# Opening of a fused attention, dense and expert kernel: y held in PSUM between quarters, a new order of single steps, and three element-wise steps moved to GpSimd

## The chip, the cores and the metric

The kernel runs on one core of a Trainium2 chip. The metric is the device time of one execution in microseconds. The engines are TensorE (PE, matrix products; PEld is its weight load), VectorE (DVE), ScalarE (ACT), GpSimd (POOL) and SyncE (SP, whose queue issues most transfers). Each engine works through its own queue in order; a wait at the head of a queue holds everything behind it on that engine.

## The reference

Three stages follow one another on 4608 tokens (8 batches of 576, 512 columns each). All inputs are fp32 except the dense weights, which arrive with eight bytes each and are read as pairs of 32-bit words.

```
kv  = einsum('bhsd,bhse->bhde', k, v)              # attention without softmax, 8 heads of 64
out = einsum('bhsd,bhde->bhse', q, kv)
x   = out / sqrt(mean(out*out) + 1e-6) * g_norm    # 4608 x 512
h   = x @ w_in                                     # 512 -> 2048
g   = max(h, 0) + alpha * min(h, 0)
y   = g @ w_out                                    # 2048 -> 512
e   = argmax(y @ w_gate);  gate = softmax(...)[e];  eom = sigmoid(y @ w_output_gate)
out = gate * eom[e] * (max(y @ w1[e], 0) @ w2[e])  # 8 experts, one for each token
```

## The kernel before

The tokens are cut into 12 blocks of 384, each of three tiles of 128 tokens. A value that feeds a product is held as two fp16 parts (a high part, and the rest as a low part), and each product is a sum of three fp16 products of parts.

The **opening** handles blocks 0 and 1 together, because the dense weights are not yet in SBUF. The weights come in 16 pieces of w_in and 16 of w_out (512 KB each), and are worked up in four **quarters** of four pieces. Each piece takes: a magnitude on ACT (`magnitude`, L493), a row maximum on DVE (`maximum`, L500, tile acc), three bit steps on DVE that build an fp32 value out of the two words (`bits`, L508, L510, L512), and, when the scale of the quarter is known, a high part on ACT (L533) and a low part on DVE (L535). The scale takes a reduction on DVE (tile amx), a transpose on PE (L152, tile allmax), a reduction on DVE (tile amrow), a product with ones on PE (L159), and a run of tiny steps on DVE (`pow2`, tiles pw_e, sig). Of a quarter's h, each of eight pieces (four for each block) takes twelve products on PE (L663), a scaled copy out of PSUM on ACT (L666, tile m), the bent line on DVE (L672, tile r), a high part on ACT (L674, tile g) and a low part on GpSimd (L675). Six **y units** follow (L686: twelve products into one PSUM bank, one for each block and tile), and ACT copies each sum out of PSUM (L716). From the second quarter on, a y unit begins with an fp32 product of the sum so far with a scaled identity, `keep` (L711), which brings the sum back into PSUM with the factor that fits the quarter's scale.

The order of the opening is written out by hand, the same on every engine: code calls the steps one after another, in larger groups (a piece's maximum and bits in one call, a whole scale in two). Behind it, the fourth quarter's y units, the routing of blocks 0 and 1 and the attention of block 2 are interleaved by the framework's scheduler.

For **later blocks** (3 to 11) attention takes, for each tile, a scaling of q by powers of two on DVE (L321, tile qs), its high part on ACT and its low part on DVE (L325), a transposing transfer (tile qT), products on PE (L347), a square on ACT, a row sum on DVE, a power -1/2 on GpSimd (L369, tile rs), a scaling on DVE (L394), and the high part (ACT, L401) and low part (DVE, L406) of x, and a transposing transfer. The k-v product of each batch is scaled in the same way (L291, tile kvsc). GpSimd also scatters the finished rows of y (L813, ytab). After block 11 the expert stage runs on tiles of tokens sorted by expert (L1140, L1162).

Of the kernel before, what the change touches and what calls it, by code (L numbers as in the profile page):

```python
# [66 lines left out]
def body(ctx: ExitStack, tc, q, k, v, g_norm, w_in, w_out, alpha, w_gate, w_og, w1, w2, out):  # L67
# [79 lines left out]
    def all_max(am, nm):  # L147
        return max_rows(max_turn(am, nm, ps_l, "l"), am.shape[1], nm)

    def max_turn(am, nm, pool_, tag):  # L150
        ps = pool_.tile([P, P + E], F32, tag=tag, name="allmax" + nm)
        pe.transpose(ps[:am.shape[1], 0:P], am, ident)  # L152
        return ps

    def max_rows(ps, n, nm):
# [18 lines left out]
    keep = const.tile([P, P], F32, name="keep")  # L174
# [42 lines left out]
    late = []  # L217

    def load_kv(n, now=False):
        if not now and late is not None:  # L220
            late.append(lambda: load_kv(n, True))
        elif n < len(kv_order):
# [11 lines left out]
    def load_q(n, now=False):  # L234
        if not now and late is not None:
            late.append(lambda: load_q(n, True))
        elif n < len(q_order):
# [24 lines left out]
    def kv_step(n, pool_=None, tag="a"):  # L262
# [4 lines left out]
        if hp % 2 == 0:  # L267
            kv_ps[b] = (pool_ or ps_a).tile([P, 2, D], F32, tag=tag, name=f"kvps_{b}_{hp}")
        ps = kv_ps[b]
# [4 lines left out]
        if hp % 2 == 1:  # L274
            for i in range(2):
                sl = slice(64 * i, 64 * i + 64)
                (act.copy if b < 2 else dve.tensor_copy)(out=kvbd[b % 2][sl, hp - 1:hp + 1, sl], in_=ps[sl])
        load_kv(n + 2 if n >= NPAIR else len(kv_order))
# [3 lines left out]
    def kv_halves(b):  # L282
# [8 lines left out]
        dve.tensor_tensor(out=t, in0=src, in1=s_.unsqueeze(2).to_broadcast([P, H, D]), op=ALU.mult)  # L291
# [5 lines left out]
    def att_parts(i):  # L297
# [6 lines left out]
        def tr(t, pool_=None, tag="a"):  # L304
# [3 lines left out]
            if split_q:  # L308
# [12 lines left out]
                dve.tensor_tensor(out=qs, in0=qv, in1=s_.unsqueeze(2).to_broadcast([P, H, D]), op=ALU.mult)  # L321
# [6 lines left out]
            else:  # L328
                qps = (pool_ or ps_a).tile([P, NPAIR, P], F32, tag=tag, name="qps" + nm)
                for hp in range(NPAIR):  # L330
                    for e in range(2):
                        pe.matmul(qps[64 * e:64 * e + 64, hp, :], qv[:, 2 * hp + e, :], ident, start=True, stop=True)
                qT[t] = at.tile([P, NPAIR, P], F32, tag="qT", name="qT" + nm)
                act.copy(out=qT[t], in_=qps)
# [3 lines left out]
        def products(t):  # L338
# [12 lines left out]
            xs = at.tile([P, DM], F32, tag="xs", name="xs" + nm, bufs=3)  # L351
# [34 lines left out]
        def scaled(t):  # L386
            nm = f"_{G}_{t}"
# [4 lines left out]
            else:  # L392
# [3 lines left out]
                              in1=rs.unsqueeze(2).to_broadcast([P, H, D]), op=ALU.mult)  # L396
            if i < 2 and t == ts[-1]:
# [6 lines left out]
        def low(t):  # L404
            xs, x16 = tiles.pop(t)
            dve.tensor_tensor(out=x16[:, 1, :], in0=xs, in1=x16[:, 0, :], op=ALU.subtract)  # L406
# [5 lines left out]
        return ts, tr, products, sums, exponents, scaled, low  # L412

    def att_steps(i):
        G = i // 3
        split_q = i >= SPLIT_Q
        ts, tr, products, sums, exponents, scaled, low = att_parts(i)

        def om(t):
            products(t)  # L420
            sums(t)
            exponents(t, t)
            scaled(t)
            low(t)
# [126 lines left out]
    def scale_out(j, am=None):  # L551
# [8 lines left out]
        else:  # L560
# [7 lines left out]
            exp_to(d[:, 1:2], d[:, 1:2], 127 << 23)  # L568
            act.activation(out=keep, in_=ident, func=AF.Copy, scale=d[:, 1:2])
        if j == NG - 1:  # L570
            d = small.tile([P, NG], F32, tag="egf", name="egf", bufs=1)
# [630 lines left out]
    with tc.manual_schedule(engines={ET.PE, ET.DVE, ET.Activation, ET.SP}):  # L1202
# [23 lines left out]
        for n in range(2):  # L1226
            kv_step(n)
# [266 lines left out]
```

## Time and profile before

| | us |
|---|---|
| median of three runs | 1390.82 (1384.95 to 1391.77) |
| the profiled execution, its own time | 1392.61 |
| its span in the trace | 1390.6 |
| PE, DVE, ACT, POOL busy in it | 1287.6, 821.6, 556.9, 251.1 |
| mean granted TensorE clock | 0.975 of 2.4 GHz |

The span is the time from the first to the last instruction; the execution's own time is 2.0 us longer. Busy shares are means over stages with different limits, so the stages are read one by one below.

### The profile page before, as it was taken

The numbers are of one execution on the slowest core, as the hardware profiler recorded it, in microseconds if no ns is written. First come the engines' busy times: TensorE is split into PE (matmuls) and PEld (weight loads), VectorE is DVE, ScalarE is ACT, GpSimd is POOL, SyncE is SP. The second block draws the span as 40 slices with busy tenths as digits, with TensorE's granted clock in tenths as the row PEclk, the third lists the DMA queues.
The fourth block names the chain that finished last, engine by engine and source line by source line (L and its number), as shares of the span: only waits on it lengthen the run. The fifth ranks groups of instructions, "written<-read, shape, count | busy, mean of one in ns | idle before, by whom it ended". The sixth has DMA issues, their size and how long they took to land. (4 is left out here: it accounts for less than half of the span.)

```text
span 1390.6 us, 21985 instructions
## 1 busy us (share of the span) xinstructions
PE 1287.6 (93%) x7717; PEld 666.1 (48%) x7717; DVE 821.6 (59%) x2386; ACT 556.9 (40%) x931; POOL 251.1 (18%) x342
## 2 busy tenths in 40 slices
PE   5688879999999999999999999999979999999995
PEld 4443435555555454545555555554434444444442
DVE  6786877867878687869697878462521221212210
ACT  3443535435556474646564656351111111111110
POOL 3212203111120102110111111101322222222110
PEclk9799999999999999999999999999989999999998
DMA  9562215646896775677846665316999799799631
GB/s 255 148 174 91 70 52 150 146 83 191 202 240 174 218 183 148 198 199 160 237 117 177 174 174 146 99 32 179 246 329 192 164 281 281 144 253 234 130 84 38
DMA packets 323297, 236.22 MB, mean 170 GB/s; under 512 B 246236, under 2 KB 279020, under 8 KB 318704
## 3 DMA queue, kind: packets, MB, share of 16 engines
q1 hardware_dynamic: 303760, 189.05, 55.3%
q0 software_dynamic: 8960, 28.91, 6.5%
q10 hardware_dynamic: 10464, 16.82, 3.8%
q8 instruction: 62, 1.02, 0.3%
q14 instruction: 51, 0.42, 0.1%
HBM read 248.34 MB, written 53.25 MB: 217 GB/s over the span
## 5 line engine op out<-in xcount | busy, mean ns | idle before, releaser
L663 PE MATMUL h<-x,wi 128*128 128x384 f16 x2304 | 406.6, 328 | 12.0 <-ACT m L666 10.1
L686 PE MATMUL y<-wo,g 128*128 128x512 f16 x1728 | 404.0, 382 | 13.6 <-ACT wo L533 5.3
L663 PEld LDWEIGHTS <-wi 128*128 128x128 f16 x2304 | 221.2, 98 | 163.9 <-issue 17.5
L686 PEld LDWEIGHTS <-g 128*128 128x128 f16 x1728 | 165.8, 98 | 210.4 <-issue 25.3
L1146 DVE CAST h_d<-br_d 128x512 f16<-128x512 f32 x62 | 27.1, 438 | 267.9 <-ACT br_d L1144 160.1
L1162 PE MATMUL bo_d<-lane,hT_d 128*128 128x512 f16 x744 | 169.4, 385 | 10.4 <-DMA hT_d<-h_d 10.4
L1140 PE MATMUL bh_d<-lane,byT_d 128*128 128x512 f16 x744 | 165.3, 379 | 0.0
L672 DVE SCALAR_TENSOR_TENSOR r<-m,alphat 128x384 f32<-128x384 f32 x192 | 119.6, 625 | 30.1 <-ACT m L666 28.9
L369 POOL TENSOR_TENSOR rs<-ms,mhalf 128x8 f32<-128x8 f32 x36 | 65.9, 1833 | 358.7 <-DVE qm L375 330.1
L674 ACT CAST g<-r 128x384 f16<-128x384 f32 x192 | 97.1, 508 | 83.9 <-DVE r L672 80.6
L1162 PEld LDWEIGHTS <-hT_d 128*128 128x128 f16 x744 | 73.4, 99 | 102.1 <-DMA hT_d<-h_d 11.4
L1140 PEld LDWEIGHTS <-byT_d 128*128 128x128 f16 x744 | 72.7, 98 | 88.1 <-issue 0.8
L666 ACT ACTIVATE m<-h,scal 128x384 f32<-128x384 f32 x160 | 91.6, 575 | 44.6 <-PE h L663 43.5
L675 DVE TENSOR_TENSOR g<-r,g 128x384 f16<-128x384 f32 x160 | 88.1, 551 | 15.3 <-ACT g L674 14.8
L454 ACT ACTIVATE whi_w<-rawe,es_w 128x1024 f16<-128x1024 f32 x64 | 71.2, 1143 | 56.0 <-DVE es_w L144 40.5
L455 DVE SCALAR_TENSOR_TENSOR wlo_w<-rawe,es_w,whi_w 128x1024 f16<-128x1024 f32 x64 | 81.0, 1278 | 20.8 <-DMA ws<-wlo_w 17.8
L1144 ACT ACTIVATE br_d<-bh_d 128x512 f32<-128x512 f32 x62 | 37.0, 597 | 131.2 <-PE bh_d L1140 109.9
L813 POOL DMA_INDIRECT ytab<-row,pos x36 | 38.8, 1077 | 277.8 <-DVE pos L794 65.9
L602 ACT ACTIVATE eab_w<-rawe 128x1024 bf16<-128x1024 f32 x64 | 67.5, 1057 | 40.6 <-DMA rawe<-in_moe_w_dram 36.9
L1165 ACT ACTIVATE ob_d<-bo_d,msc_d 128x512 f32<-128x512 f32 x31 | 21.3, 687 | 143.2 <-PE bo_d L1162 143.2
L1166 POOL DMA_INDIRECT out_dram<-ob_d,oidx_d x31 | 32.5, 1050 | 215.8 <-ACT ob_d L1165 208.9
L675 POOL TENSOR_TENSOR g<-r,g 128x384 f16<-128x384 f32 x32 | 32.9, 1032 | 146.0 <-ACT g L674 146.0
(350 smaller groups left out, 1284.9 us busy)
## 6 DMA issues: line engine op xcount, KB each, us to landing
lane<-ws SPq DMA_DIRECT2D x150, 1024.0 KB
rawe<-in_moe_w_dram SPq DMA_DIRECT2D x64, 512.0 KB
ws<-whi_w ACTq DMA_DIRECT2D x64, 256.0 KB
ws<-wlo_w SPq DMA_DIRECT2D x64, 256.0 KB
rawwi<-in_moe_w_in_dram SPq DMA_DIRECT2D x16, 512.0 KB
q<-in_q_dram SPq DMA_DIRECT2D x16, 512.0 KB
rawwo<-in_moe_w_out_dram SPq DMA_DIRECT2D x16, 512.0 KB
k<-in_k_dram SPq DMA_DIRECT2D x28, 256.0 KB
```

The source lines that it names most:

```text
L369: pool.tensor_tensor(out=rs, in0=ms, in1=mhalf, op=ALU.pow)
L454: act.activation(out=dst_h, in_=src, func=AF.Copy, scale=s)
L455: dve.scalar_tensor_tensor(out=dst_l, in0=src, scalar=s, in1=dst_h, op0=ALU.mult, op1=ALU.subtract)
L602: act.activation(out=ab.rearrange("p a b -> p (a b)"), in_=raws[4 * m + i], func=AF.Abs)
L663: pe.matmul(ps, wi[:, f // 4 * NC + c, w, fs], xt[i][:, xc, :], start=(n == 0), stop=(n == 3 * NC - 1))
L666: act.activation(out=r0, in_=ps, func=AF.Copy, scale=(scst if start else scal)[:, f:f + 1])
L672: dve.scalar_tensor_tensor(out=r, in0=r0, scalar=alphat[:, f:f + 1], in1=r0, op0=ALU.mult, op1=ALU.max)
L674: act.copy(out=hi, in_=r)
L675: (pool if start else dve).tensor_tensor(out=lo, in0=r, in1=hi, op=ALU.subtract)
L686: pe.matmul(ps, g[:, t, f % GF, us], wo[:, f, w, :], start=(start and m == 0), stop=(stop and m == 2))
L1140: pe.matmul(hp[ts], j["yT"][:, x, ts], w1_[:, w, c, hs], start=(m == 0), stop=(m == 3 * NC - 1))
L1162: pe.matmul(po[ts], hT[:, g, ts], w2_[:, w, f, :], start=(m == 0), stop=(m == 3 * NFE - 1))
```

## The change

Four things change.

- **y in PSUM.** The six y sums of blocks 0 and 1 get a PSUM bank each from the first quarter on (three of the pool of attention, two of the pool of y, one of the small pool). The products of the next quarter add to what stands there. Between quarters ACT scales a bank in place (`y_scaled`, F). The products with `keep` and the copies between quarters are gone; one copy (L1376 of the changed kernel) remains after the fourth quarter. h takes turns in two fixed banks.
- **Order.** The opening is a list of some 470 words, each a single step, issued in the order of the list. Quarters use g tiles 2, 3 and 0, 1 in turn. Attention of both blocks 0 and 1 stands ahead of the first h products.
- **Loads.** All of k, v and q of the first tiles stand ahead of the first weight in SP's queue.
- **GpSimd.** For every block from 3 on, the scaling of q, the low part of x, and for every batch from 2 on the scaling of the k-v product, go from DVE to GpSimd.

```
-        ps = ps_y.tile([P, DM], F32, tag="y", name=f"y_{i}_{j}_{u}")
-        if j:
-            pe.matmul(ps, keep, acc[:, u, :], start=True, stop=False)
+        if j == 0:
+            pool_, tag = ((ps_a, "a"), (ps_y, "y") if u < 2 else (ps_l, "l"))[i]
+            ybank[i, u] = pool_.tile([P, DM], F32, tag=tag, name=f"y_{i}_{u}")
         for f in range(j * GF, (j + 1) * GF):
-            y_products(ps, g, f, u, j == 0 and f == 0, f == (j + 1) * GF - 1)
+            y_products(ybank[i, u], gs2[j, i], f, u, f == 0, f % GF == GF - 1,
+                       skip_group_check=True)
             if j == NG - 1:
                 tick()
-        act.copy(out=acc[:, u, :], in_=ps)
+
+    def y_scaled(i, j, u):
+        act.activation(out=ybank[i, u], in_=ybank[i, u], func=AF.Copy, scale=kfac[:, j:j + 1])
...
-            act.activation(out=keep, in_=ident, func=AF.Copy, scale=d[:, 1:2])
+            exp_to(kfac[:, js], d[:, 1:2], 127 << 23)
...
-                dve.tensor_tensor(out=qs, in0=qv, in1=s_.unsqueeze(2).to_broadcast([P, H, D]), op=ALU.mult)
+                pool.tensor_tensor(out=qs, in0=qv, in1=s_.unsqueeze(2).to_broadcast([P, H, D]), op=ALU.mult)
...
-            dve.tensor_tensor(out=x16[:, 1, :], in0=xs, in1=x16[:, 0, :], op=ALU.subtract)
+            (dve if i < SPLIT_Q else pool).tensor_tensor(out=x16[:, 1, :], in0=xs, in1=x16[:, 0, :], op=ALU.subtract)
...
-        dve.tensor_tensor(out=t, in0=src, in1=s_.unsqueeze(2).to_broadcast([P, H, D]), op=ALU.mult)
+        pool.tensor_tensor(out=t, in0=src, in1=s_.unsqueeze(2).to_broadcast([P, H, D]), op=ALU.mult)
...
+    plan = """
+    f0 f1 N0 Li0 Li1 Li2 N1 Li3 Lo0 n4 n5 k0 k1 k2 K1 Ai0 q0 Mi0 Bi0 Ai1 q1 Q0 k3 Q1 N2 Mi1 Lo1 Ai2 Bi1 q2 K3
...
+    G132 R031 Y122 G031 Y121
+    """
...
+        for word in plan.split():
+            emit(word)
...
+            y_scaled(i, NG - 1, u)
+            y_unit(i, NG - 1, u)
+            act.copy(out=accs[i][:, u, :], in_=ybank[i, u])
```

In the list, L, A, M, B, S and T are load, magnitude, maximum, bits, high and low part of a weight piece (i for w_in, o for w_out); U, u, V, v, W are the five steps of a scale; H, C, R, G are products, copy, bend and split of an h piece (block, quarter, number); Y and F are a y unit and its scaling (block, quarter, tile).

**SP, the start of the program.** These rows are SP's first loads before the change (wi stands in for k and v at this time, rawwi is a weight piece, q_0 the first q):

```order
L255 DMA wi<-in_k_dram 64x8x64
L258 DMA wi<-in_k_dram 128x4x256
L255 DMA wi<-in_v_dram 64x8x64
L258 DMA wi<-in_v_dram 128x4x256
L478 DMA rawwi_238<-in_moe_w_in_dram 128x1024
L258 DMA wi<-in_k_dram 128x4x256
L258 DMA wi<-in_v_dram 128x4x256
L478 DMA rawwi_242<-in_moe_w_in_dram 128x1024
L242 DMA q_0_244<-in_q_dram 128x8x128
L478 DMA rawwi_246<-in_moe_w_in_dram 128x1024
```

And these are the first of the changed program:

```order
L244 DMA wi<-in_k_dram 64x8x64
L247 DMA wi<-in_k_dram 128x4x256
L244 DMA wi<-in_v_dram 64x8x64
L247 DMA wi<-in_v_dram 128x4x256
L247 DMA wi<-in_k_dram 128x4x256
L247 DMA wi<-in_v_dram 128x4x256
L231 DMA q_0_264<-in_q_dram 128x8x128
L492 DMA rawwi_266<-in_moe_w_in_dram 128x1024
L492 DMA rawwi_268<-in_moe_w_in_dram 128x1024
L492 DMA rawwi_270<-in_moe_w_in_dram 128x1024
```

The first weight piece moves from fifth to eighth place, behind the second half of k and v and the first q, and three weight pieces now follow each other.

**DVE, the scale of w_in's second quarter.** Before the change, the row reduction (amrowwi) is followed at once by the first step that needs PE's product with ones (pw_ewi):

```order
L1221 TENSOR_REDUCE amxwi_1287<-accwi_1224 128x1
L508 TENSOR_SCALAR cwi_1306<-uwi_1284 128x512
L510 SCALAR_TENSOR_TENSOR cwi_1306<-rawwi_1100,cwi_1306 128x512
L512 SCALAR_TENSOR_TENSOR wo<-rawwi_1100,cwi_1306 128x512
L157 TENSOR_REDUCE amrowwi_1327<-allmaxwi_1289 1x1
L132 TENSOR_SCALAR pw_ewi_1330<-allmaxwi_1289 128x1
L135 TENSOR_SCALAR pw_ewi_1330<-pw_ewi_1330 128x1
```

In the changed program the same two steps (amrowi, and pw_ewi from an h bank) stand eight rows apart:

```order
L1261 TENSOR_REDUCE amrowi_887<-hbank_671 1x1
L696 SCALAR_TENSOR_TENSOR r_3_889<-m_3_839,alphat 128x384
L549 SCALAR_TENSOR_TENSOR wo<-wi,sogs,wo 128x512
L514 TENSOR_SCALAR uwo_891,accwo_880<-uwo_891 128x512
L696 SCALAR_TENSOR_TENSOR r_0_915<-m_0_897,alphat 128x384
L522 TENSOR_SCALAR cwo_917<-uwo_891 128x512
L524 SCALAR_TENSOR_TENSOR cwo_917<-rawwo_831,cwo_917 128x512
L526 SCALAR_TENSOR_TENSOR wi<-rawwo_831,cwo_917 128x512
L132 TENSOR_SCALAR pw_ewi_936<-hbank_671 128x1
L135 TENSOR_SCALAR pw_ewi_936<-pw_ewi_936 128x1
```

Two bends of h and the bits of a w_out piece now stand between the reduction and the step that waits for PE.

**POOL, the first later block.** Before the change GpSimd has only the powers (rs) and the scatter of y's rows (ytab, row) around block 3:

```order
L369 TENSOR_TENSOR rs_8_2120<-ms_8_2118,mhalf 128x8
L369 TENSOR_TENSOR rs_0_2670<-ms_0_2668,mhalf 128x8
L813 DMA ytab<-row_193,pos_2362 36864x528
L813 DMA ytab<-row_194,pos_2362 36864x528
L810 COPY row_193<-ids 128x1
L813 DMA ytab<-row_195,pos_2362 36864x528
L810 COPY row_194<-ids 128x1
```

In the changed program the scalings (kvsc, qs) and the low part of x (x_1_0) stand among them:

```order
L375 TENSOR_TENSOR rs_8_2043<-ms_8_2041,mhalf 128x8
L285 TENSOR_TENSOR kvsc_2170<-kvbd_205,kvs_2157 128x512
L327 TENSOR_TENSOR qs_0_2365<-q_0_1970,qsc_0_2358 128x512
L327 TENSOR_TENSOR qs_1_2458<-q_0_1970,qsc_1_2451 128x512
L327 TENSOR_TENSOR qs_2_2645<-q_2_2023,qsc_2_2638 128x512
L843 DMA ytab<-row_193,pos_2282 36864x528
L375 TENSOR_TENSOR rs_0_2589<-ms_0_2587,mhalf 128x8
L843 DMA ytab<-row_194,pos_2282 36864x528
L840 COPY row_193<-ids 128x1
L415 TENSOR_TENSOR x_1_0_2599<-xs_0_2580,x_1_0_2599 128x512
```

The scatter of block 0's rows now stands behind four element-wise steps, and the low part of x stands behind a wait for a scattered row.

## Rows read from the trace of the kernel before

**Rows 1.** Windows, four stages: length, then each engine's busy us (instructions), clock, DMA, GB/s

```profile
0.00:213.70 213.70, 161.52 (x956) 91.02 (x957) 157.62 (x377) 95.06 (x174) 45.64 (x86) 0.91 0.46 130
213.70:247.40 33.70, 31.68 (x258) 17.88 (x257) 24.80 (x75) 16.04 (x28) 8.09 (x6) 1.00 0.58 157
247.40:960.00 712.60, 690.19 (x4490) 374.24 (x4491) 537.53 (x1666) 373.29 (x612) 104.93 (x108) 1.00 0.64 168
960.00:1390.60 430.60, 404.22 (x2018) 182.93 (x2015) 101.69 (x271) 72.51 (x117) 92.42 (x143) 0.97 0.81 193
```

**Rows 2.** Windows within the opening; columns PE, PEld, DVE, ACT, POOL as above

```profile
0.00:11.20 11.20, 3.02 (x29) 2.28 (x30) 4.10 (x26) 1.93 (x2) 5.90 (x50) 1.00 0.78 221
...
116.20:164.40 48.20, 39.63 (x187) 19.51 (x187) 35.61 (x77) 21.38 (x40) 8.24 (x8) 0.96 0.27 88
164.40:213.70 49.30, 41.32 (x198) 20.61 (x198) 39.05 (x89) 22.97 (x42) 9.76 (x10) 0.97 0.15 49
```

**Rows 3.** Waits in the opening, 0 to 213.7: total us, times, longest

```profile
DVE r L672 <- ACT m L666: 15.1, 9, 5.6
DVE pw_ewi L132 <- PE allmaxwi L159: 14.4, 2, 7.3
...
PE allmaxwi L152 <- DVE amxwi L1221: 12.4, 4, 5.3
...
DVE uwi L500 <- ACT uwi L493: 5.5, 3, 3.4
...
DVE uwo L500 <- ACT uwo L493: 4.6, 2, 2.5
```

**Rows 4.** Timeline of DVE, second quarter of w_in: start, us, [idle before, releaser]

```profile
132.17 0.27 DVE L157 TENSOR_REDUCE amrowwi<-allmaxwi 1x1 f32<-1x128 f32 x1
139.71 0.16 DVE L132 TENSOR_SCALAR pw_ewi<-allmaxwi 128x1 int32<-128x1 int32 x1 [7.27 <-PE allmaxwi L159]
```

**Rows 5.** Timeline of PE at the same place

```profile
136.61 2.75 PE L686 MATMUL y<-wo,g 128*128 128x512 f16 x12
139.29 0.38 PE L159 MATMUL allmaxwi<-amrowwi,ones 1*128 1x1 f32 x2
```

**Rows 6.** Groups by line: PE in the opening, ACT in the last stage (PSUM source)

```profile
L711 PE MATMUL y<-g,keep 128*128 128x512 f32 x24 | 14.2, 679 | 0.0
...
L1165 ACT ACTIVATE ob_d<-bo_d,msc_d 128x512 f32<-128x512 f32 x31 | 21.3, 687 | 143.2 <-PE bo_d L1162 143.2
```

**Rows 7.** DMA rate in 40 slices of 0 to 215; DVE's first weight step

```profile
GB/s 129 303 352 297 273 222 173 288 231 231 9 2 99 222 236 383 86 3 105 188 98 3 0 129 208 53 0 111 181 102 0 0 156 212 24 3 0 0 0 142
...
11.26 0.69 DVE L500 TENSOR_SCALAR_CACHE_REDUCE uwi<-uwi 128x512 f32<-128x512 f32 x1 [0.27 <-ACT uwi L493]
```

**Rows 8.** GpSimd's 384-column low part; a DVE step beside it, and alone

```profile
L675 POOL TENSOR_TENSOR g<-r,g 128x384 f16<-128x384 f32 x30 | 30.9, 1032 | 142.4 <-ACT g L674 142.4
...
120.70 0.92 POOL L675 TENSOR_TENSOR g<-r,g 128x384 f16<-128x384 f32 x1 [1.70 <-ACT g L674]
...
120.72 1.18 DVE L508 TENSOR_SCALAR cwi<-uwi 128x512 int32<-128x512 int32 x1
...
127.79 0.43 DVE L508 TENSOR_SCALAR cwi<-uwi 128x512 int32<-128x512 int32 x1
```

**Rows 9.** The middle, 247.4 to 960: DVE groups that move, POOL's waits, PE's waits

```profile
L406 DVE TENSOR_TENSOR x<-xs,x 128x512 f16<-128x512 f32 x27 | 18.5, 686 | 4.0 <-ACT x L401 3.9
L321 DVE TENSOR_TENSOR qs<-q,qsc 128x512 f32<-128x512 f32 x27 | 18.4, 683 | 0.0
...
POOL ytab L813 <- DMA ytab<-row,pos: 35.4, 13, 4.2
...
PE h L663 <- ACT m L666: 7.6, 8, 2.1
PE ops L347 <- DMA qT<-q: 5.2, 4, 1.9
PE y L686 <- ACT g L674: 4.6, 3, 3.9
```

**Rows 10.** Timeline of PE around the start of block 2

```profile
215.30 1.09 PE L332 MATMUL qps<-ident,q 128*64 128x128 f32 x16
...
236.92 1.09 PE L350 MATMUL ops<-kvbd,qT 128*64 128x128 f32 x16
...
247.38 0.82 PE L663 MATMUL h<-x,wi 128*128 128x384 f16 x4 [1.91 <-DMA x<-x]
```

More of the change, by code (lines that the diff above doesn't have):

```diff
@@ L173, in body @@
         "sig", "isig", "sog", "isog", "scol", "crow"))
[L174 removed]
+    kfac = const.tile([P, NG], F32, name="kfac")
     eg = const.tile([P, NG], F32, name="eg")
@@ L215, in body, with load_kv @@
     q_order = [(G, t) for G in range(B // 2) for t in (0, 2, 4, 6, 8)]
[L217 to L222, printed above, removed]
+    def load_kv(n):
+        if n < len(kv_order):
             b, hp = kv_order[n]
@@ L232, in load_kv, with load_q @@
                 kv_in[nm, n] = t
[L234 to L237, printed above, removed]
+    def load_q(n):
+        if n < len(q_order):
             G, t = q_order[n]
@@ L328, in tr @@
             else:
[L329 to L334, printed above, removed]
+                turned(t)
+                turned_copy(t)
             if t % 2 == 1 or t == 8:
@@ L410, in low @@
                                    in_=x16.rearrange("p a b -> p (a b)"))
-        return ts, tr, products, sums, exponents, scaled, low
+        return ts, dict(q=turned, Q=turned_copy, t=tr, p=products, P=squares, s=sums, e=exponents, x=scaled, X=high, z=low,
+                        Z=x_turned)
     def att_steps(i):
@@ L416, in att_steps @@
         split_q = i >= SPLIT_Q
-        ts, tr, products, sums, exponents, scaled, low = att_parts(i)
+        ts, do = att_parts(i)
+        tr = do["t"]
         def om(t):
[L420 to L424, printed above, removed]
+            for what in "pPs":
+                do[what](t)
+            do["e"](t, t)
+            for what in "xXzZ":
+                do[what](t)
         nxt = {0: 2 * G + 1, 1: None, 2: 2 * G + 2}[i % 3]
@@ L669, in h_unit, with h_bend @@
     def h_unit(f, g, start, part):
+        h_split(f, g, start, h_bend(f, part))
+    def h_bend(f, part):
         i, r0 = part
@@ new lines, in body, with weights, scales @@
+    ybank, hbank, held = {}, [], {}
+    dense = dict(i=din, o=dout)
+    parts = {}
+    for i in range(2):
+        ts, do = att_parts(i)
+        for t in ts:
+            parts[t] = do
+    def weights(what, d, n):
+        if what == "L":
+            d.load(n)
+        elif what == "A":
+            d.magnitude(n)
+        elif what == "M":
+            d.maximum(n)
+        elif what == "B":
+            d.bits(n)
+        else:
+            d.split(n, "ST".index(what))
+    def scales(what, w, j):
+        d, nm = dense[w], f"{w}{j}"
+        if what == "U":
+            held[nm] = small.tile([P, 1], F32, tag="amx", name="amx" + nm)
+            dve.tensor_reduce(out=held[nm], in_=d.acc, axis=AX.X, op=ALU.max)
+        elif what == "u":
+            if j:
+                ps = hbank["io".index(w)][:, BLK:BLK + P]
+            else:
+                ps = ps_l.tile([P, P], F32, tag="l", name="allmax" + nm)
+            pe.transpose(ps[:1, :], held[nm], ident)
+            held[nm] = ps
+        elif what == "V":
+            m = small.tile([E, 1], F32, tag="amrow", name="amrow" + nm)
+            dve.tensor_reduce(out=m[:1], in_=held[nm][:1, :], axis=AX.X, op=ALU.max)
+            held[nm] = held[nm], m
+        elif what == "v":
+            ps, m = held[nm]
+            held[nm] = ps[:, 0:1]
+            pe.matmul(held[nm], ones32[:1, :], m[:1], start=True, stop=True)
+        else:
+            (scale_in, scale_out)["io".index(w)](j, held.pop(nm))
@@ L1217, in body @@
         dve.tensor_tensor(out=sgp, in0=gp, in1=sal, op=ALU.mult)
-        def top(d, nm):
-            m = small.tile([P, 1], F32, tag="amx", name="amx" + nm)
-            dve.tensor_reduce(out=m, in_=d.acc, axis=AX.X, op=ALU.max)
-            return max_turn(m, nm, ps_l, "l")
-        (t0, t1, t2), tr, products, sums, exponents, scaled, low = att_parts(0)
-        din.magnitude(0)
-        for n in range(2):
-            kv_step(n)
-        din.build(0)
-        din.magnitude(1)
-        for n in range(2, NPAIR):
-            kv_step(n)
```

325 lines of the change are left out of this document (123 added, 202 removed).

## The prediction

> **What bounds the kernel now.** I read the windows by stage first. From 247 us to 960 us PE is busy 690.2 of 712.6 us, and in the last stage 404.2 of 430.6 us; there PE is the bound, and little is left to win [rows 1]. In the opening (0 to 213.7 us, the last h product) no engine is the bound: PE is busy 161.5, DVE 157.6 and ACT 95.1 of 213.7 us [rows 1]. Quarters of it look alike: 48 to 49 us long with 40 to 41 us of PE and 36 to 39 us of DVE [rows 2]. So PE and DVE, both in order, wait for each other in turn, and the list of waits says where. DVE waits 15.1 us in sum for ACT's copies of h, 14.4 us for PE's product with ones, 5.5 and 4.6 us for magnitudes; PE waits 12.4 us for the reductions of w_in's scales [rows 3]. One place shows the mechanism. DVE finishes the row reduction at 132.4 us and stands still for 7.27 us until PE's product with ones [rows 4]; that product takes 0.38 us, but stands behind y units in PE's queue and starts at 139.29 us [rows 5]. Before that PE had itself waited for DVE. It is an order of steps that costs here, more than the work.
>
> **The new order.** I build the new end of the opening from DVE, the engine whose work hardly changes. All its steps of the opening stay in it, so 157.6 us of busy time remain [rows 1]. To it come:
>
> - *The start.* DVE now has 4.1 us of work before its first weight step at 11.26 us [rows 2, 7]. In the new order of loads the first weight has 2.9 MB before it in SP's queue (k and v of batch 0 with 2.36 MB, q with 0.52 MB) instead of 1.3 MB, so that it ends at 3.4 MB. The rate row gives 0.7 MB in the first 5.4 us, 2.3 MB after 10.8 us, and then 352 GB/s [rows 7], so 3.4 MB are there at 13.9 us; with about 1 us of landing and 0.7 us of magnitude DVE starts at about 15.6 us. Idle before: 15.6 - 4.1 = 11.5 us (7.1 before). In return three pieces follow each other at about 1.5 us, less than the 2.6 us that DVE takes for one, so that the 5.5 us of waiting for early magnitudes goes.
> - *The named waits.* 15.1, 14.4 and 4.6 us, 34.1 us in sum [rows 3]. In the new list the step after the reduction is eight DVE rows later, and a bend stands several steps behind its copy. PE is left with 147.3 us of work, under 80% of the new length, so that its queue has slack. What survives lies between nothing and all 34.1 us; I take a fifth, 7 us, near the low end, because both big waits are of the kind that other work between two steps covers.
> - *The small rest.* Idle time of DVE before is 213.7 - 157.6 = 56.1 us; less 7.1 us at the start and 39.6 us of named waits (with the 5.5) there remain 9.4 us, which I keep.
> - *GpSimd beside a denser DVE.* A DVE step beside GpSimd's low part took 1.18 us, and 0.43 us alone [rows 8]: 0.75 us for such a meeting. 32 of them make 24 us at most; DVE pays for those that meet now, 74% of the time busy, and is to be busy 85%: some 11% of 24, so 2 to 3 us more; I take 2.
>
> The sum is 157.6 + 11.5 + 7 + 9.4 + 2 = 187.5 us, 26.2 us less than 213.7. PE's own bound is no tighter: 161.5 us less the 24 halves of the `keep` products, 14.2 us [rows 6], is 147.3 us, and 9 us of start.
>
> **y in PSUM.** The twelve `keep` products within the opening are in that sum. ACT gets 18 scalings and six copies in place of 24 copies; a scaled copy out of PSUM of the same shape took 0.69 us [rows 6]; in place into PSUM the trace shows nothing, and I put it between 0.5 and 0.9 us. That is 9 to 16 us of ACT, which is busy 95 of 187 us; a y unit waits for its own scaling only when the unit before it in the same bank has just ended, and each bank has five other units between. I cost it at nothing; if that cover is gone, a unit waits 0.9 us, 16 us in all.
>
> **The start of block 2.** The six `keep` products of the fourth quarter (12 halves of 0.68 us, 8 us at the opening's mean [rows 6]) go as well. But attention of block 2 needs a bank of the pool that now holds y of block 0. Its first turn started at 215.30 us, three products into the last quarter; the last products of attention began at 236.92 us, and h of block 2 at 247.38 us, 33.7 us after the opening and 10.5 us after those products [rows 10]. In the new PE order the first turn stands behind 35 products of y (8.0 us of the fourth quarter's units at 2.75 us [rows 5]). Then follow 22 products (5.0), two small groups (2.1), 15 products (3.4), two groups (2.1), about 1 us of waiting, the last products (1.1), and the same 10.5 us: with 1.1 us for the first turn, 34.3 us. So what `keep` frees here, PE waits for x instead: plus 0.6 us.
>
> **The middle.** DVE gives 27 scalings of q and 27 low parts away, 18.4 and 18.5 us [rows 9], and six scalings of k-v. GpSimd's row for 384 columns is 0.92 to 1.03 us [rows 8], so 512 columns are 1.2 to 1.4 us, 60 of them 73 to 83 us on an engine that is busy 105 of 712.6 us [rows 1]. Each is 0.5 to 0.7 us later than on DVE, and holds a DVE step that meets it up by up to 0.75 us; at DVE's 75% this gives 60 x 0.75 x 0.75, about 34 us, of the 41 us back. DVE is not the bound, and attention runs a block ahead. So zero, between two ends: at best PE's waits behind ACT (7.6 and 4.6 us) go, at worst each of 27 tiles has PE wait 0.7 us longer where it waits 5.2 us now [rows 9], 19 us.
>
> Of this move the Trainium skill has a rule, in "GPSIMD Engine Reference", sections "Elementwise", "Engine selection" and "Key points": element-wise work with two inputs belongs on VectorE, GpSimd being about half as fast, and the two contend when a VectorE step has two SBUF inputs or runs in a two-port mode. The 1.18 us beside 0.43 us agrees [rows 8]. Its 2.6 cycles for an element at 1.2 GHz would make 512 columns 1.1 us, an estimate, and the 60 steps 67 us; the sum would stay.
>
> **Sum.** 1392.6 us of the profiled execution, less 26.2, plus 0.6, is 1367.0 us. The median of the three runs is 1.8 us below the profiled execution, so 1365 us.
>
> **Rivals.**
>
> 1. *Half of the waits stay* (chance 0.2). The list is fixed, and the chip's jitter on transfers or a late copy of h stops an in-order queue as before; PE now has fewer idle slots in which to be late. If 20 of the 34.1 us survive, 13 more: 1378 us. For it: nine waits for copies are spread over the whole opening [rows 3]. Against it: the largest waits have one cause each [rows 4, 5].
> 2. *Better than that* (chance 0.15). No named wait survives (-7), the small ones halve (-5), and PE's waits behind ACT in the middle mostly go (-5): 1348 us. For it: DVE would be at 92% in the opening, no more than PE reaches later; against it: two in-order engines at 80% and more rarely never meet.
> 3. *GpSimd makes it slower than before* (chance 0.07). In GpSimd's queue the low part of x stands behind waits for scattered rows (35.4 us of them, up to 4.2 us each [rows 9]), and the scatter behind scalings that wait for q. If x and qT of later blocks come late, PE waits in the middle, where every microsecond counts. Over 27 tiles 1.2 us for each make 33 us and bring 1365 to 1398 us. It decides from about 1 us per tile on. For it: PE already waits for qT four times. Against it: a block's attention has the y products of the block before, some 30 us, as cover.
> 4. The forecast as built has what is left, 0.58.
>
> That the order does nothing is no rival: with all 34.1 us surviving, the end of the opening is at 214.6 us, and 1392 us come out.
>
> **Numbers.** Range 1346 to 1384 us: the low end near rival 2, the high end takes rival 1 and 6 us of surviving waits or late x more. About 0.5%, 7 us, is what a measurement of this kernel can tell from no change. The forecast, rival 2 and nearly all of rival 1 lie below 1384; rival 1's upper part and some of rival 3 lie within 7 us of 1391; the rest of rival 3 is slower: 0.87, 0.07, 0.06.
>
> **What would show it.** The opening's last product ends at about 187 us (180 to 200), with DVE 82 to 88% busy in it; no wait of pw_e for PE over 2 us; DVE's first weight step at 15 to 16 us; no L711; scalings of about 0.7 us. h of block 2 starts some 34 us later, with 5 to 7 us of PE waiting for x. In the middle PE's idle stays 15 to 30 us, and GpSimd shows 60 steps of 1.2 to 1.4 us. The prediction is wrong if the opening ends after 200 us (then the list meets waits that I don't see), if the start of block 2 is late by 40 us, or if PE's idle in the middle passes 40 us.

## The result, and the profile after

The changed kernel takes 1374.08 us (median of four runs, 1372.97 to 1374.83), the kernel before 1390.21 us beside it. The ratio is 0.989 (95% interval 0.9863 to 0.9917): faster by 16 us, against 26 forecast. The profiled execution took 1372.97 us, its span 1371.3. One execution of the run e2 below fell into a slower state (1430.92 us, at a granted clock of 0.927 against 0.965 to 0.974 in the others) and is left out of its figures.

The windows by stage come first, of the changed kernel. The opening is cut at the end of its 36th product of y in the row below that starts at 184.12 (the last y unit of the third quarter), which ends the work that before ended with the last h product at 213.7; the rest is cut as in [rows 1], with one difference. For both kernels the middle now ends at the first expert product (on tile byT_s), since the round number 960 of [rows 1] has no counterpart here.

```profile
0.00:192.00 192.00, 151.41 (x933) 88.67 (x934) 161.72 (x389) 95.86 (x176) 51.29 (x88) 0.90 0.54 154
192.00:227.71 35.71, 27.65 (x247) 16.86 (x245) 21.33 (x65) 14.12 (x24) 4.91 (x3) 0.86 0.51 116
227.71:951.87 724.16, 698.56 (x4511) 378.34 (x4511) 539.06 (x1602) 374.35 (x612) 180.69 (x168) 0.99 0.62 165
951.87:1371.30 419.43, 398.16 (x1991) 180.40 (x1989) 101.34 (x270) 72.60 (x117) 91.39 (x143) 0.98 0.80 199
```

The kernel before, with the same cut:

```profile
247.38:964.18 716.80, 694.39 (x4516) 376.22 (x4517) 537.74 (x1667) 373.29 (x612) 104.93 (x108) 1.00 0.63 167
964.18:1390.60 426.42, 400.04 (x1991) 180.97 (x1989) 101.50 (x270) 72.51 (x117) 92.42 (x143) 0.97 0.81 195
```

So the opening became 21.7 us shorter (213.7 to 192.0), the way to block 2 2.0 us longer, the middle 7.4 us longer, and the last stage, where nothing was changed, 7.0 us shorter: -19.3 us of span. The last stage took 418.4 to 429.7 us in the profiles of this study, whatever the kernel, so its 7 us can't be put down to the change.

The waits of DVE in the opening, the counterpart of [rows 3] (total us, times, longest):

```profile
DVE pw_ewi L132 <- PE allmaxi L1266: 3.8, 1, 3.8
DVE uwi L514 <- ACT uwi L507: 3.5, 1, 3.5
...
DVE pw_ewi L132 <- PE hbank L682: 1.3, 1, 1.3
DVE pw_ewo L132 <- ACT m L687: 1.1, 1, 1.1
```

Of the 34.1 us of named waits 6.2 are left (3.8, 1.3, 1.1); DVE is busy 161.7 of 192.0 us. The next rows are the scalings in PSUM that fall into the opening (14 of 18), and then PE's timeline around the start of block 2, as [rows 10]:

```profile
L746 ACT ACTIVATE y<-y,kfac 128x512 f32<-128x512 f32 x14 | 8.8, 654 | 0.0
```

```profile
184.12 15.49 PE L713 MATMUL y<-wo,g 128*128 128x512 f16 x71
199.54 1.09 PE L304 MATMUL qps<-ident,q 128*64 128x128 f32 x16
...
213.34 1.09 PE L352 MATMUL ops<-kvbd,qT 128*64 128x128 f32 x16 [0.39 <-ACT qT L308]
...
221.03 1.12 PE L262 MATMUL kvps<-v,k 128*64 128x64 f32 x16 [4.06 <-DMA v<-in_v_dram]
...
227.71 1.76 PE L682 MATMUL h<-x,wi 128*128 128x384 f16 x5 [0.44 <-DMA x<-x]
```

In the middle, GpSimd's groups that came (busy us, mean ns | idle before):

```profile
L327 POOL TENSOR_TENSOR qs<-q,qsc 128x512 f32<-128x512 f32 x27 | 38.8, 1445 | 37.9 <-DVE qsc L144 18.0 <-issue 17.9 <-ACT kv L288 2.1
...
L415 POOL TENSOR_TENSOR x<-xs,x 128x512 f16<-128x512 f32 x27 | 33.5, 1241 | 86.7 <-ACT x L410 59.7 <-issue 22.9 <-DVE kexp L643 4.0
...
L285 POOL TENSOR_TENSOR kvsc<-kvbd,kvs 128x512 f32<-128x512 f32 x6 | 6.7, 1122 | 60.1 <-DVE qsc L144 32.1 <-DVE sr L144 16.9 <-DVE kvs L144 11.1
```

Sixty steps left DVE, and its busy time stayed (537.7 to 539.1 us). What PE waits for there has changed, though, against [rows 9]. Before, the wait for yT was 3.0 us (the first row), that for qT 5.2, and that behind ACT's g 4.6. In the changed kernel (the other rows) the wait for yT has grown, and the one behind ACT's g is gone.

```profile
PE l L747 <- DMA yT<-row: 3.0, 3, 1.7
```

```profile
PE l L777 <- DMA yT<-row: 11.4, 5, 4.6
PE ops L349 <- DMA qT<-q: 6.9, 7, 2.6
PE h L682 <- ACT m L687: 5.4, 5, 1.7
```

### The profile page after: what moved, and what is told of

It is laid out like the page before. It is cut to its first block, busy times and chain, and to the rows that moved or that the text cites. A ratio compares the mean times of both kernels' runs of the same rounds, so it can differ in the third digit from the quotient of the medians.

```text
span 1371.3 us, 21907 instructions
## 1 busy us (share of the span) xinstructions
PE 1275.8 (93%) x7678; PEld 664.3 (48%) x7678; DVE 823.5 (60%) x2325; ACT 556.9 (41%) x928; POOL 328.3 (24%) x402
## 5 line engine op out<-in xcount | busy, mean ns | idle before, releaser
L682 PE MATMUL h<-x,wi 128*128 128x384 f16 x1920 | 341.4, 329 | 6.0 <-ACT m L687 5.4
L469 DVE SCALAR_TENSOR_TENSOR wlo_w<-rawe,es_w,whi_w 128x1024 f16<-128x1024 f32 x64 | 86.3, 1366 | 33.3 <-DMA ws<-wlo_w 23.9
L702 DVE TENSOR_TENSOR g<-r,g 128x384 f16<-128x384 f32 x160 | 91.1, 572 | 18.3 <-ACT g L701 17.6
L682 PE MATMUL hbank<-x,wi 128*128 128x384 f16 x384 | 69.1, 341 | 12.8 <-ACT g L701 6.4
L1195 ACT ACTIVATE ob_d<-bo_d,msc_d 128x512 f32<-128x512 f32 x31 | 21.3, 687 | 140.8 <-PE bo_d L1192 140.8
```

What stands on the lines that cost most here:

```text
L469: dve.scalar_tensor_tensor(out=dst_l, in0=src, scalar=s, in1=dst_h, op0=ALU.mult, op1=ALU.subtract)
L682: pe.matmul(ps, wi[:, f // 4 * NC + c, w, fs], xt[i][:, xc, :], start=(n == 0), stop=(n == 3 * NC - 1))
L702: (pool if start else dve).tensor_tensor(out=lo, in0=r, in1=hi, op=ALU.subtract)
```

## The experiments

Theory: the new order ends the two engines' mutual waits, so that DVE's work sets the opening's length; the move to GpSimd changes nothing in the middle. Rivals: the opening gained by the removed `keep` products of PE; the move costs, by late results or by the hold between GpSimd and DVE. Beside the experiments the kernel before had medians of 1393 to 1395 us, 3 to 5 above its 1390, so ratios count. "Moves undone" is the run e1 below. Opening ends are those of the 36th product, as above; before the experiments' own edits it was 192.0 us in the first profile, and 190.2 to 190.9 in others with the same opening.

**The move to GpSimd, undone and alone.** e1_mid_back is the changed kernel with this edit, at all three places (L285, L327, L415); e2_mid_alone is the kernel before with the reverse.

```
-                pool.tensor_tensor(out=qs, in0=qv, ...)
+                dve.tensor_tensor(out=qs, in0=qv, ...)
```

> The changed kernel with the sixty later steps (27 query scalings, 27 low parts of x, 6 key-value scalings) back on VectorE, so that only the opening is new. Theory (the mutual hold of VectorE and GpSimd gives back what the move takes away, and TensorE sets the pace there): the middle stays at 713 us within 3, VectorE's busy time in it stays within 8 us of 537, the whole within 3 us of 1374. Rival 1 (the move is part of the gain): the middle becomes 5 us or more longer, the whole 1379 or more. Rival 2 (GpSimd's steps of 1.2 to 1.4 us delay the turned x and q; TensorE's waits for yT are 11.4 us there against 3.0 before): the middle becomes 5 us or more shorter, the whole 1369 or less.

> The kernel before with the same sixty steps on GpSimd and nothing else changed. Theory (the opening alone makes the difference): 1390 within 3 us, the opening's end at 213.7 within 1 us. Rival 1 (the move saves): 1385 or less. Rival 2 (the move costs): 1395 or more.

e1: 1367.93 us, ratio 0.9808 (0.9771 to 0.9844), faster than both kernels: the interval lies under the changed kernel's 0.9863 to 0.9917. e2: 1405.93 us (median of nine), 1.0064 (1.0032 to 1.0096), slower than the kernel before. By these two runs the move costs: 0.64% of 1394, 9 us, in e2 (11.5 by the medians), and 11 us between e1 and the control below (10 by the ratios). The theory of no effect fell for the kernel before; how much the move costs in the changed kernel is less certain, as the table at the end of these experiments shows. The middles say less than the whole times, too. In e1 it is 720.6 us long: 3.6 less than in the changed kernel, where Rival 2 asked for 5 or more, and still 3.8 more than in the kernel before. In e2 it is 731.6, 14.8 more than before, and the opening, though unedited, ended 1.8 us later. PE's waits in the middle, of e1 and then of e2:

```profile
PE h L682 <- ACT m L687: 9.4, 7, 2.9
PE ops L349 <- DMA qT<-q: 6.5, 7, 2.8
PE y L713 <- ACT g L701: 3.3, 4, 2.0
PE l L777 <- DMA yT<-row: 2.2, 2, 1.5
```

```profile
PE l L747 <- DMA yT<-row: 12.6, 7, 4.0
PE ops L347 <- DMA qT<-q: 6.1, 6, 3.6
```

The wait for yT goes with the move: 5.8 to 12.6 us in the six profiles that have all of it (5.8 in e13, below, which has another order), 2.2 to 3.6 in five that have none of it (before, e1, e10, e12, e14). One stands against this: e11, below, has no step of it on GpSimd, and 9.9 us. The scheduler orders the middle anew for each kernel, so its order has a part in these waits.

**The changed kernel again, and the move in halves.** c_changed is a control. e8_low_back puts only the low parts of x back on DVE, e9_low_alone only the scalings of q and k-v.

```
-            (dve if i < SPLIT_Q else pool).tensor_tensor(out=x16[:, 1, :], ...)
+            dve.tensor_tensor(out=x16[:, 1, :], ...)
```

> The changed kernel itself, beside the three below, because times of the kernel before stood 4 us higher beside the first four runs than in its own runs. Both theories: ratio to before about 0.989 as before; TensorE's waits for yT in the middle 7 to 13 us.

> The changed kernel with only the 27 low parts of x back on VectorE; the 27 query scalings and 6 key-value scalings stay on GpSimd. Theory (a low part on GpSimd comes late, the transposition of x stands waiting for it at the head of SyncE's queue, 142 us in sum against 30 us behind VectorE, and the transpositions of yT are queued behind it): SyncE's wait for x is under 60 us, TensorE's waits for yT fall from 11.4 us to 2 to 4 us, and nearly the whole difference to the run with all three moves undone (6 us) is had: the whole 4 to 7 us under the changed kernel beside it. Rival (the scalings, or contention with VectorE in general, cost): within 2 us of the changed kernel, yT waits still 7 us or more.

> The counterpart: the changed kernel with the 27 query scalings and 6 key-value scalings back on VectorE, the low parts of x alone on GpSimd. Theory: SyncE's wait for x stays over 100 us, TensorE's waits for yT stay at 7 to 13 us, the whole within 3 us of the changed kernel beside it. Rival: yT waits of 2 to 4 us and a whole 4 to 7 us under the changed kernel.

c_changed: 1379.13 us, 0.988 (0.9819 to 0.9941), an interval that overlaps e1's by a little. e8: 1370.93, 0.9837 (0.9773 to 0.9902). e9: 1369.67, 0.9822 (0.9761 to 0.9882). By the medians either half put back returns most, but the intervals overlap. The waits speak against my guess that the low part of x is the culprit: in e9 it stays on GpSimd, and SP waits for it as long as ever (141.9 us in the changed kernel, 153.9 here), while PE's waits for yT and qT are short.

```profile
SPq L421 <- POOL x L415: 153.9, 26, 21.6
```

```profile
PE l L777 <- DMA yT<-row: 4.0, 4, 1.9
PE ops L349 <- DMA qT<-q: 3.4, 6, 1.2
```

e8, with the scalings on GpSimd, still has 6.2 and 7.9 us there. This points to the scaling as what comes late, but doesn't show it: the profile of e9 is of its fastest execution, 1359.85 us, 8 us or more under its other four. The place is seen best at the longest wait of the changed kernel: POOL, SP and PE around 450 to 471 us.

```profile
452.35 0.99 POOL L843 DMA_INDIRECT ytab<-row,pos  x1 [1.73 <-DMA ytab<-row,pos]
...
455.82 1.03 POOL L327 TENSOR_TENSOR qs<-q,qsc 128x512 f32<-128x512 f32 x1
```

```profile
456.88 0.37 SPq L231 DMA_DIRECT2D q<-in_q_dram  x1
...
461.25 2.74 SPq L764 DMA_TRANSPOSE yT<-row  x1
```

```profile
470.89 0.40 PE L777 MATMUL l<-wg,yT 128*128 128x32 f16 x8 [4.63 <-DMA yT<-row]
```

The scaling stands in GpSimd's queue behind the scatters of finished rows and ends at 456.85 us. DVE had its factors (qsc) ready at 452.18 us, so it began 3.6 us late; on DVE, in e1, it begins 0.2 us behind them. The next load of q needs the buffer that the scaling reads, and starts at 456.88; the transposition of yT is behind that load in SP's queue. With the scaling on DVE (e1, where block 2 starts 1.5 us earlier) both are 4.5 to 6 us earlier, and PE doesn't wait for yT:

```profile
450.77 0.37 SPq L231 DMA_DIRECT2D q<-in_q_dram  x1
...
456.76 3.31 SPq L764 DMA_TRANSPOSE yT<-row  x1
```

**The queue's order.** e13_queue_order keeps the move, and calls the load of q after the products of its tile and the transposition of x one step later.

```
-            if t % 2 == 1 or t == 8: load_q(n + 2)        # in tr(t)
+            ... the same call behind products(t); Z(t) one step after om(t)
```

> The changed kernel with all sixty steps on GpSimd, and only the order of SyncE's queue changed in the middle: the next load of q stands behind the products of its tile instead of behind its scaling, and the transposition of x one step of attention later, behind what other steps issue. Theory (the transpositions of yT and qT are late because they stand behind those two in the queue): SyncE's waits for GpSimd fall from 190 us in sum to under 90, TensorE's waits for yT from 7 to 13 us to 2 to 4 us, and the whole is 6 us or more under the changed kernel (1372 or less beside a before of 1394). Rival (the lateness of the results themselves, or the mutual hold): waits and time within 3 us of the changed kernel (1379 beside a before of 1394).

1374.51 us, 0.9835 (0.9767 to 0.9903); yT 5.8 us, qT 2.3. SP still waits 142.0 us for x and 59 for qs (141.9 and 62 in the changed kernel), and around 455 us its row still has the load of q ahead of the transpositions of yT and qT: the framework's scheduler, and not the order of calls, sets SP's row in the middle. The time lies between the two cases and its interval holds both, so this run doesn't decide between them.

**GpSimd's load without its results.** Two runs with the moves undone and sixty steps of GpSimd added, each a 128x512 subtraction that nothing reads. In e11_idle_steps they read constants.

```
+    pool.tensor_tensor(out=junk, in0=ident.unsqueeze(1).to_broadcast([P, 4, P]), in1=junk, op=ALU.subtract)
```

> All sixty steps back on VectorE, and at the same sixty places GpSimd does a 128x512 subtraction with two inputs into a tile of its own that nothing reads: the load of GpSimd and its meetings with VectorE as in the changed kernel, but no result that comes late. Its steps ahead of it still put off what stands behind them in GpSimd's queue. Theory (what costs is that transpositions and loads stand in SyncE's queue behind results of GpSimd): TensorE's waits for yT in the middle stay at 2 to 4 us, the whole within 4 us of the run with the moves undone (1368 us beside a before of 1394). Rival (the mutual hold of VectorE and GpSimd costs, whoever reads the results): 8 us or more above that run, 1376 or more beside a before of 1394.

1411.8 us, 1.0124 (1.0064 to 1.0185). Nothing held these steps back, so GpSimd did them all from 7.7 to 132 us, in the opening: not what I meant, but a sharper test of it. Windows of the opening, e11 and then e1:

```profile
0.00:220.30 220.30, 154.60 (x933) 86.76 (x934) 197.73 (x391) 96.42 (x177) 131.58 (x149) 0.88 0.47 134
```

```profile
0.00:190.25 190.25, 151.12 (x933) 87.42 (x934) 161.69 (x389) 95.63 (x176) 51.11 (x88) 0.91 0.55 156
```

80.5 us of GpSimd beside the opening made the same DVE steps 36.0 us longer, 0.60 us for each of sixty, and the opening ended 30.0 us later. The middle of e11, by then free of idle steps, was 733.8 us long, 13 more than in e1; no run here shows the cause. In e14_copies_in_place each idle step reads tiles of the real one, so that it runs beside it.

```
+    pool.tensor_tensor(out=junk, in0=xs, in1=x16[:, 0, :], op=ALU.subtract)   # behind DVE's low part; likewise for qs, kvsc
```

> The run before last but two had its sixty idle steps of GpSimd run ahead into the opening, since nothing held them back. Here each of them reads two tiles of the step that VectorE does (the scaled q and its high part, x and its high part, the scaled k-v and its high part), so that it runs when that step does; it writes a tile that nothing reads, and all sixty real steps are on VectorE. Theory (late results at the head of SyncE's queue cost): SyncE's waits for GpSimd in the middle are none, TensorE's waits for yT 2 to 4 us, the whole within 4 us of the run with the moves undone (1368 beside a before of 1394). Rival 1 (the mutual hold costs): VectorE's busy time in the middle 20 to 40 us over 536, TensorE's waits for ScalarE and for yT longer, the whole 8 us or more above that run. Rival 2 (both): between.

1383.25 us, 0.9916 (0.9883 to 0.9949): 15 us over e1. Between the two profiles, 19.8 us apart, 10.0 us lie in the middle and 9.3 in the last stage, where nothing differs. The windows of the middle of e14 and of e1, and e14's wait for yT:

```profile
226.79:957.35 730.56, 702.67 (x4511) 378.57 (x4511) 577.43 (x1662) 373.56 (x612) 190.46 (x168) 0.99 0.61 163
```

```profile
226.23:946.81 720.58, 698.03 (x4512) 377.00 (x4511) 535.91 (x1662) 372.98 (x612) 104.01 (x108) 0.99 0.63 165
```

```profile
PE l L783 <- DMA yT<-row: 2.9, 3, 1.6
```

Rival 1 came out in part. DVE is busy 41.5 us more for the same steps (20 to 40 forecast), 0.69 us for each idle step; that is what such a step costs on DVE itself (0.68 to 0.69 us in [rows 9]). But PE's waits for ACT's m and g fell, from 12.7 to 9.3 us, and yT is at 2.9 us, as the theory said of a run without late results. What grew are PE's waits for DVE's own results (0.8 to 4.9 us) and for qT (6.5 to 9.1). So the load of GpSimd lengthens DVE's work by itself. It is not the changed kernel's case, though: there DVE gave 41 us away and got them back, here it has its own steps and the price. The 15 us are no measure of what the move costs.

**What sets the opening's length.** e6_pe_load gives PE its old work back, e7_dve_load gives DVE more; sums and values stay as they were.

```
+        for n in range(TB + 1 if 0 < j < NG - 1 else 0):      # e6, in y_unit; nil is a zero tile
+            pe.matmul(ybank[i, u][:, n * P:(n + 1) * P], nil, ident, start=False, stop=False, ...)
```
```
+            for _ in range(2 if i < 2 * GF else 1):               # e7, the last of the bit steps
                 dve.scalar_tensor_tensor(out=self.value(i).bitcast(I32), in0=lo, scalar=29, ...)
```

> The changed kernel with TensorE work about as large as the removed products with the diagonal tile put back: each y unit of the second and third quarter first adds four products of a zero tile with a 128x128 f32 tile into its bank, 12 units, about 14 us of TensorE altogether (24 halves at 0.59 us before); the sums stay what they were. No copy and no wait of the old form comes back. Theory (VectorE sets the opening's length, TensorE is idle 40 us of its 192): the opening ends 0 to 4 us later, the whole 1374 to 1378. Rival (the gain of the opening was the TensorE work removed): the opening ends 10 to 14 us later, the whole 1384 to 1388.

> The changed kernel with 16 more VectorE steps of 0.69 us in the opening: for the first eight tiles of either weight the last step that builds the value is done twice, which leaves the value as it was; 11.0 us of VectorE altogether. Theory (VectorE sets the opening's length, with 95% of it busy from 41 us on): the opening ends 9 to 12 us later, the whole 1383 to 1386. Rival (the steps lie in waits for other engines): 0 to 4 us later, the whole 1374 to 1378.

e6: 1391.07 us, 0.9973 (0.9947 to 0.9998); e7: 1389.26, 0.9958 (0.9933 to 0.9983). Their openings:

```profile
0.00:197.00 197.00, 157.36 (x1029) 97.08 (x1030) 162.56 (x394) 99.02 (x180) 51.25 (x89) 0.93 0.53 150
```

```profile
0.00:197.86 197.86, 150.97 (x933) 86.92 (x934) 172.68 (x407) 96.41 (x177) 51.21 (x88) 0.91 0.52 150
```

Against the 190.2 to 192.0 us without the edit, 11.0 us of DVE cost 6 to 7.6 us, 13.0 us of PE products 5 to 6.8. Both forecasts missed: neither engine alone sets the length. Which weighs more the runs don't tell. PE as a whole is busy only 6.0 to 6.2 us longer in e6 than in the changed kernel and e1, because the new products overlap with their neighbours and others ran faster, at a granted clock of 0.93 against 0.90 and 0.91. And 2.6 us of e6's delay come from the three y units behind its last h product, where PE is busy without a gap in the changed kernel, too. If the 14.2 us of `keep` counted in the old order as these products do here, removing them was worth some 6 of the 22 us, an estimate. That the order made the rest is argued, not shown: no run has the old order without `keep`. The whole times rose by more, 12 us (e6) and 10 us (e7) over the control. In the profiles, e6's middle was long (733.4 us against 724.2 and 727.9 in two of the changed kernel); e7's was not (726.8), but its last stage took 429.7 us. No run shows why.

**An earlier start.** e10_early_back and e12_early_late_gate have the moves undone, loads of weights alternating with k, v and q, the gates' maximum out of the first reduction, and the first magnitude ahead of the first k-v copies.

```
- f0 f1 N0 Li0 Li1 Li2 N1 Li3 Lo0 n4 n5 k0 k1 k2 K1 Ai0 q0 Mi0 Bi0 ...
+ f0 Li0 f1 Li1 N0 Li2 N1 Li3 Lo0 n4 n5 k0 k1 Ai0 Mi0 Bi0 k2 K1 q0 ...
```

> All three moves undone, and in the opening an earlier start: the gates' maximum has a reduction of its own behind the first weight step and so no longer stands ahead of the first one, loads of weights alternate with those of k, v and q as in the kernel before, the first magnitude stands ahead of ScalarE's first copies of k-v, and the two steps of the first scale's turn stand ahead of the next two q turns. Theory (the opening is bound by VectorE and what it waits for in its first 40 us): VectorE's first weight step at 11 to 14 us instead of 17.9, no wait of 3.8 us for the scale at 33 us, the opening's end 4 to 7 us earlier than with the moves undone alone (whole some 10 us under the changed kernel beside it). Rival (TensorE's dependencies later in the opening set its end whatever VectorE does early): the end less than 2 us earlier.

> The run with the early start again, but the gates' maximum and its scale now stand some 35 steps later, in single steps with others between, because in that run VectorE waited 4.0 us for TensorE's product of it and lost what the start had gained (first weight step at 11.3 us instead of 17.5, opening's end only 2.3 us earlier). Theory (VectorE's early waits move the end): no wait over 2.5 us of VectorE from 18 to 60 us, the opening's end 4 to 7 us earlier than with the moves undone alone (the last 71 products of y in the opening begin at 176 to 179 us against 182.4). Rival (data or TensorE sets the pace there): at 180 us or later.

e10: 1372.68 us, 0.985 (0.9789 to 0.9911); e12: 1376.72, 0.9874 (0.9824 to 0.9924). DVE's first weight step came at 11.3 and 11.9 us instead of 17.5, but the 71 products began at 180.15 and 181.85 against 182.41 in e1. DVE only moved its wait, as the third step of e12 shows:

```profile
11.85 0.69 DVE L514 TENSOR_SCALAR_CACHE_REDUCE uwi<-uwi 128x512 f32<-128x512 f32 x1 [0.73 <-ACT uwi L507]
16.37 0.69 DVE L514 TENSOR_SCALAR_CACHE_REDUCE uwi<-uwi 128x512 f32<-128x512 f32 x1 [1.91 <-ACT uwi L507]
22.14 0.69 DVE L514 TENSOR_SCALAR_CACHE_REDUCE uwi<-uwi 128x512 f32<-128x512 f32 x1 [3.17 <-ACT uwi L507]
24.67 0.68 DVE L514 TENSOR_SCALAR_CACHE_REDUCE uwi<-uwi 128x512 f32<-128x512 f32 x1
```

The fourth stands at 24.67 us, in e1 at 25.04. The theory fell: the late first step costs the opening 0.6 to 2.3 us.

**The price of the move, over all runs.** e10 and e12 undo the move as e1 does. Put beside the runs that keep it (lengths in us, from the profiles; ratios to the kernel before):

| run | steps moved | middle | last stage | ratio |
|---|---|---|---|---|
| before | 0 | 716.8 | 426.4 | 1 |
| e1 | 0 | 720.6 | 418.6 | 0.9808 |
| e10 | 0 | 724.3 | 421.7 | 0.985 |
| e12 | 0 | 722.2 | 425.0 | 0.9874 |
| changed kernel | 60 | 724.2 | 419.4 | 0.989 |
| c_changed | 60 | 727.9 | 429.4 | 0.988 |
| e13 | 60 | 722.1 | 423.6 | 0.9835 |

e12, without the move, is no faster than the control with it, and e13, with all of it, is faster than e12 by the medians; their intervals overlap. So in the changed kernel the price lies somewhere between nothing and 11 us. The runs don't show more than that, since the order of the middle differs from kernel to kernel. What e1, e10 and e12 do show is that the opening alone makes the kernel faster, and e2 that the move alone doesn't.

## Why the prediction was right in direction and 9 us short

- *The opening's end.* 187.5 us forecast, 192.0 measured (190.2 to 190.9 in later profiles). The waits went as forecast: of 34.1 us of named ones 6.2 are left, and DVE is 84% busy. The terms: DVE's work 161.7 instead of 157.6 + 2, surviving waits 6.2 instead of 7, the start 13.1 us of idle instead of 11.5, the small rest 11.0 instead of 9.4. Two signs failed: one wait of pw_e took 3.8 us, not under 2, and the first weight step came at 17.9 us, not at 15 to 16. Its magnitude starts at 17.18 us, right behind ACT's copy of the k-v product, for which ACT had waited for PE until 15.34 us; the second weight piece was there at 18.30. The sum had 13.9 us and 1 us of landing, which no row gives. What was wrong in kind is the sentence that PE's bound is no tighter: in e6 13.0 us of PE products moved the end by 5 to 6.8 us.
- *y in PSUM.* The scalings took 654 ns, within 0.5 to 0.9, and no row of PE's waits names them. Right.
- *The start of block 2.* 34.3 us forecast, 35.7 measured, and the closeness is partly luck. The sum counts the last products of attention twice: the 10.5 us of [rows 10] run from their start, so that 33.2 us come out. They began 21.3 us after the opening (22.7 in the sum), and h came 14.4 us after that. Of the 5 to 7 us of waiting for x only 0.4 came; 4.06 us of waiting for v was not foreseen.
- *The middle.* "So zero" is the step that failed: 7.4 us between the two profiles, within the bounds of -12 and +19 that it gave. Not all of them are the move's: e1, without it, keeps 3.8, and e10 and e12 keep 7.5 and 5.4. The give-back was put at 34 of 41 us; DVE got all of it back (537.7 us busy before, 539.1 after), and e14 shows the price to be 0.69 us a step, so that nothing was freed. Then the lateness: I looked at GpSimd's queue and at x, and wrote that y's products cover a late x. They do (PE waits 0.4 us for x). But the loads of q and the transpositions of yT stand in SP's queue behind results of GpSimd, and that queue I did not follow. Rival 3 had the direction, with the wrong tile and 33 us instead of 11 at most.
- *The sum.* Between the two profiled executions the forecast was off by 4.5 us in the opening, 1.4 in the start and 7.4 in the middle, less the 7.0 of the last stage: 6.3. The other 3 us are the step from profile to median: the forecast took 1.8 us off for it, but the changed kernel's profile was 1.1 us under its median. The 7.0 us of the last stage are luck; without them the forecast would have been some 13 us short between the profiles.

The Trainium skill, "GPSIMD Engine Reference", section "Engine selection", keeps element-wise work with two inputs on VectorE. The runs agree: 1.0064 with the move alone. The Trainium skill, "SBUF — State Buffer", section "SBUF: two separate sides", says of a VectorE step with two SBUF inputs (or in a two-port mode) and a GpSimd step that reads SBUF that whichever starts first holds the shared ports for its whole instruction. The runs agree in kind: beside idle steps with a mean of 1.3 to 1.5 us DVE lost 0.60 to 0.69 us a step, less than the whole step on the mean, and as much as the move saves.

Not settled: how much the move costs in the changed kernel (nothing to 11 us), and how that divides between late results and the scheduler's new order of the middle. e13 changed little in the queue, and a middle with the old order and the steps on GpSimd wasn't tried. Nor is it settled how the opening's 22 us divide between the order and the removed `keep`. What the hold does is settled: it takes back what the move saves.

## What to carry to other kernels

Moving an element-wise step with two inputs from a busy VectorE to GpSimd beside it can free nothing: compare VectorE's busy time before and after, not the list of its steps. Where an operation moves to another engine, follow every transfer that waits for its result or its buffer, and what stands behind that transfer in the issuing queue. When two in-order engines wait for each other, add known work to each in turn and see how much of it shows in the end; take as added what the engine's whole busy time grew by, and not only the length of the new steps.

## What the runs showed of the hardware

The hold was larger than expected: sixty idle 128x512 steps of GpSimd cost DVE 36.0 us in the opening and 41.5 in the middle, 0.60 and 0.69 us each; their own length was 1.1 to 1.6 us in the opening and 1.1 to 2.4 in the middle. It doesn't fall on all steps alike. In the opening of e11 GpSimd is busy 56.4 of the 70 us from 30 to 100, while DVE does the low part of x (two inputs in SBUF) and the scaling of x (one of its two inputs is attention's product in PSUM) six times each. First e1, then e11:

```profile
L415 DVE TENSOR_TENSOR x<-xs,x 128x512 f16<-128x512 f32 x6 | 4.1, 683 | 1.6 <-ACT x L410 1.6
...
L399 DVE TENSOR_TENSOR xs<-ops,rs 128x512 f32<-128x512 f32 x6 | 4.1, 691 | 0.3
```

```profile
L419 DVE TENSOR_TENSOR x<-xs,x 128x512 f16<-128x512 f32 x6 | 7.9, 1321 | 0.0
...
L403 DVE TENSOR_TENSOR xs<-ops,rs 128x512 f32<-128x512 f32 x6 | 4.2, 692 | 0.3
```

The low part went from 683 to 1321 ns, the scaling stayed at 691 to 692.

A wait of PE can cost more than its length. Windows of the changed kernel around the 4.63 us wait for yT (the last three columns are clock, DMA, GB/s):

```profile
465.00:470.00 5.00, 1.26 (x8) 0.55 (x6) 4.24 (x14) 3.17 (x4) 0.00 (x0) 1.00 1.17 228
470.00:475.00 5.00, 3.92 (x28) 2.51 (x29) 4.96 (x11) 3.54 (x7) 2.19 (x2) 0.54 1.10 348
475.00:480.00 5.00, 5.00 (x39) 2.90 (x38) 2.88 (x11) 2.75 (x5) 0.26 (x1) 0.78 1.18 272
480.00:485.00 5.00, 5.00 (x31) 2.85 (x30) 5.00 (x15) 1.89 (x5) 1.38 (x1) 1.00 1.11 160
```

After PE had been busy 1.26 of 5 us, the granted clock was 0.54 and 0.78 for two windows, near the lower of its two levels (1.2 GHz, 0.5) in the first. Twelve products of attention behind the wait took 1.46 us; twelve at the same place took 0.84 us in e1, where PE hadn't waited for yT and the clock was 1.00:

```profile
471.80 1.46 PE L349 MATMUL ops<-kv,qT 128*128 128x128 f16 x12 [0.20 <-DMA qT<-q]
```

```profile
466.76 0.84 PE L349 MATMUL ops<-kv,qT 128*128 128x128 f16 x12
```

Of the middle's 7.4 us, 4.2 are PE busy for longer with the same products (694.4 to 698.6 us), and 3.2 are idle. The 4.2 us can't be put down to the move: e1, with 2.2 us of waiting for yT, has 698.0 us of PE, too.
